# Chunk-selected attention and gated FFN on one core: keys of two heads and rows of a half turned by one DMA each, chunk rows for the last batch only, a new order table

## The chip, the cores and the metric

The kernel runs on one core of a Trainium2 chip. The metric is the device time of one execution in microseconds. Three runs of the kernel before gave 314.94, 315.1 and 316.24 us (median 315.1).

## The reference

Four batches of 8 heads, 768 positions, head dimension 64. The keys of a head are cut into 24 chunks of 32. For each query a bound on its score with each chunk is formed from the chunk's elementwise minimum and maximum; the query keeps the 6 chunks with the largest bounds among those that are causally allowed, and attends to them only. The result of all heads is one row of 512 per position (3,072 rows), which goes through an RMS norm and a gated feed-forward layer with 1,536 hidden units.

```python
k_min = np.min(k_chunks, axis=3)
k_max = np.max(k_chunks, axis=3)
ub = np.sum(np.maximum(q[:, :, :, None, :] * k_min[:, :, None, :, :],
                       q[:, :, :, None, :] * k_max[:, :, None, :, :]), axis=-1)
ub = np.where(causal, ub, -1000000000.0)
top_chunks = np.argsort(ub, axis=-1)[..., -top_k:]
...
scores = np.where(mask, scale * np.matmul(q, k.transpose(0, 1, 3, 2)), -1000000000.0)
attn = softmax(scores)                 # along the keys
x = (attn @ v), heads side by side     # 3072 x 512
xn = x / rms * rms_g
g, val = xn @ w_gate, xn @ w_val
return (g * sigmoid(g) * val) @ w_out
```

(The softmax, the product with `v` and the sigmoid are shortened here.)

## The kernel before

The kernel first makes a list of 1,975 steps (`add`), each with the engines that may run it, the steps it depends on and the buffers that it opens or uses. `order.run` then emits them in the order of the written-out table `ORDER`, whose tokens are step numbers, with a letter where the step runs on another engine than its first choice (`a` ScalarE, `v` VectorE, `g` GpSimd). So every engine's queue, and the sync engine's DMA queue too, is in the order of that table, and nothing passes anything else on its own engine. `SLOTS` says how many buffers of a kind there are.

Heads go in pairs: 16 pairs, four to a batch, pairs 0 to 3 being batch 0. Positions go in tiles of 128, six to a head (`NT`), in two halves of three tiles.

Pairs 0 to 3 are prepared by `early`, the others two at a time by `late`. `late` gets its keys in one of two ways:

- `direct` (batch 1, pairs 4 to 7): the keys come in natural rows (`nat`), TensorE transposes them in fp32 (`turn`, L488, 6 transposes of 128 x 128 a pair), an engine copies the result out of PSUM to `kt`, VectorE reduces it to minimum and maximum of each chunk (`bounds_of`, L675 and L677), `ku` gets their difference, and casts put the transposed keys into the key set `kes` (L269).
- `chunked` (batches 2 and 3, pairs 8 to 15, from `CHUNKED` = 8 on): a second load brings the keys of four heads as one row per chunk (`kc`, L711, 768 KB); VectorE folds the rows down to minimum and maximum (L722, L732); TensorE turns the small result (`kt<-kk`, L749). The keys themselves are laid out as bf16 in `kb` by GpSimd (`kN`, L269) and turned into `kes` by two DMA transposes, one a head (`turned`, L660).

The table of `kb` has one buffer; its gaps hold the rows that add the chunk bias to the score matmul. `qn` is the same for the queries: VectorE writes the chosen chunks into its gaps (`sel`, L540), and two DMA transposes a pair (L660, `qs<-qn`) turn it. The scores `sc` (L859) of a pair wait for its queries and keys; ScalarE takes the exponential (`pt`, L876), GpSimd masks, TensorE multiplies with the values (`av`, L895), VectorE divides (`xb`).

`norm` works on a half of a batch, three tiles of rows. ScalarE or VectorE sums the squares, GpSimd takes the power (`root`). In batches 1 and 2 ScalarE scales a row block into `xf` (L981), which shares two buffers `ob` with the output tiles `osb`, and GpSimd multiplies with the gains (`xs`, L986); in batches 0 and 3 VectorE does both (`xs`, L972). Each `xs` is a bf16 tile of 128 x 512. In batch 0 TensorE transposes it; in the others one DMA transpose for each `xs` (L1000) writes it into `xT`, laid out so that 384 positions stand side by side for each group of 128 features.

`ffn` on a half: 12 gate steps (L1046) and 12 val steps (L1066) of four matmuls 128 x 384 each, which wait for all of the half's `xT`; `tanh` on ScalarE (L1053), two products on VectorE, and 9 output steps `po` (L1086) of four matmuls. `osb` goes out by a DMA on the sync queue (L1101). The weights come by DMAs that GpSimd issues. 48 `busy` matmuls on zeros fill TensorE's waits near the start.

Of the kernel before, what the change touches and what calls it, by code (L numbers as in the profile page):

```python
# [25 lines left out]
    86 134 0 66 54 3 25 12 11 67 50 59 19 58 89 28 55 24 52 38 137 42 133 85 68 69 181 62 63 229 182  # L26
    5 135 7 27 56 64 87 53 2 60 61 230 206 110 207 90a 1 111 99a 98a 18 100a 74 139 136a 51 183 71v
    254 255 73v 76 46 77 70v 138a 88a 26 144g 141 142 148a 145g 94 45 93 231 143g 158 72v 149 147g
    30 184a 189 95g 96g 40 150 190 22 101 13 75a 192a 232a 97a 91 193g 185 102 103 233 104g 241a 6
    208 151 37 237 65 44 146a 186a 234a 112 195a 196a 47 113a 105 240g 9 119a 152g 238 244a 20 210  # L30
    211a 191g 153 106 209a 154 219a 155g 117 197 156 199 114 107g 108 239g 198 120g 157v 115a 245
    109v 629 622 623 619 630 246 620 626 247 615 616 242a 608 609 215a 194g 200g 41 201 140g 159 34
    212 202 627 624 256 257a 612 203g 204 248g 16 605 48 116 606 621 122a 213 258 33 160 205v 631
    161a 249 123g 613 118g 625 124 250 628 243a 251g 92g 187 214g 640 281 252 235 29 260 165 216a
    167g 126 317 125 263a 32 633 617 261 253v 49 15 259a 127g 643 641 267a 644 607 164 657 162 610
    262g 654 311 296 632 168g 658 188g 220 128 614 130g 634 636 650 163v 221 129 655 647 637 651
    266g 642 611 131 121g 289 222 635 645 132v 166g 648 171a 638 639 282 10 283a 618 172-174 409 670
    290a 664 667 671 169g 31 78 674 668 23 345 646 223g 236g 652 360 175g 656 285 659 672 661 649
    665 666 683 677 675 680 176 662 684 36 678 681 264g 318 178g 320 319a 224 669 660 663 177 179
    284 4 321a 653 170g 17 180v 1270a 381 682 1271a 685 268 709 673 679 287 676 218g 226g 710 312  # L40
    1269a 690 21 225 693 227 686 269 270 79 314 694 8 315a 703 304 704 43 696 305a 700 695 706 265g
    691 288 291 228v 687 271g 217g 297 692 313v 729 701 688 697 1272 272 1273 711 689 80 410 735 732
    730 726 14 733 707 727 705 1280 1274 1281 39 698 713 1277 736 1282v 273 274g 708 298a 722 1275
    723 286g 702 719 1278 1276v 737 731 720 338g 716 1279v 728 375 734 275 307 717 712 721 1308 276a
    724 714 1298 310 303 699 752 81 1309 755 738 1293 753 300 756 761 1294 302 295 294 299 754 715
    301g 1310 758 762 1299 292 718 725 82 1300 757 1288 745 763 759 746 742 1303 1295 748 1304 749
    277 83 760 346 306 308g 353 739 764 1305 347a 354a 1289 349 1296 1291 309 743 1301 356 1297 747
    348 1302 750 293g 740 744 741 751 322a 316a 57 1358a 1359a 352 355 1290 1306 1311 1312 1307 1283
    1284 1286 323 351 1292 1360a 1318 1285 1338 1361 1339 1328 1319 1329 325 1323 1324 1287 368 1362
    369a 357g 324 1333 361 1363 1366 1367 1340 326g 1325 1364 1365a 1334 1330 1331 84 1368v 1320  # L50
    1332 1321 1369 1326 1327 1341 1316 1370 373 327 1313 1342 1371a 1336 328 1314 334 329 331g 330g
    332 1315 1322 1317 1335 1395 335 359 333 1372 1392 1373 1375 1397 337g 362a 1337 1393 1417 1374
    1418 1382 1383 1394 1376 1398 1385 384 385a 1396 364 1399 1419 1384 336 382 374 363 358 1377
    1387 1380 1348 1343 1386 1349 1388 1378 1379 411 383a 376 378 278g 370 1381 386a 377a 1389 1350
    365g 350g 379a 380a 395g 340 1344 371 412 372g 773 1351a 413 774 786 769 779 790 770 787 803 776
    425 771 1345 777 279 804 280g 387 805 780 772 791 800 1346a 781 792 801 388 797 778 798 775 431
    794 795 765 766 1412 802 782 788 783 1413 367 389 428 429a 426 434 435a 390v 391 793 427a 767
    799 339 839 784 1414 796 840 417 818 392 832 414g 402g 789 806 398 366 393 768 475 833 394g 834
    819 432 433a 807 808 430a 1400 1401 809 785 459 397 824 396 821 1420 825 836 1415 815 816 399
    1421 1390 1391 810 1407 817 826 837 341 1416 822 838 418g 1408 828 842 811 829 845 401g 846 400  # L60
    1409 820 843 1402 1403 460 812 478 415 830 841 416a 884 436v 1404 1405 823 479a 813 847 1352 476
    477a 403 844 831 342g 835 848 343 849 404 814 874 875 525 827 1406 437 885 876 1347 438 850 439
    860 445g 863 864 405 461 866 1353 861 853 867 851 440g 441 865 878 854 879 862 870 868 1410 886
    871 887 881 888 1422 1411 882 880 480a 462 855 481 929 877 889 852 442 531 930 883 857 858 1427
    1423 1424 912 913 926 856 923 924 344g 419 872 420 859 873 443 444g 447 446 1354 869 902 908 448
    927 914 452g 909 1355 903 920 915 895 1356a 931 1425 890 463 925 896 905 916 921 904 1430 897
    917 891 918 1432 906 1426 1428 899 922 1357 892 928 900 406g 919 1429 893 1433 910 509 898 894
    1431 907 901 1434 1437 954 1435a 1436 449 464g 465 941 958 484 932 965 495g 421 911 1449v 451g
    1448a 482 407 450 1447a 959 1450 485v 1438 944 947 942 966 1451 1452 955 483v 486v 1453 1439 948
    528 454 466v 960 943 945 526 937 1455 1456 962 1440v 956 938 963 487 964 1458 961 1441 1536a 933  # L70
    510 532 455 529v 489 1459 946 488 534 1454 533a 957 934 939 1442 950 968 951 971 1443 511 408g
    512 949 535a 972 940 1444 967 527v 935 936 422g 1457 490g 1460 467 952 953 969 491 1537a 970
    456v 973 1481 424 492 1445a 493 1494 1538a 1539 1540 1516-1518 494g 1491 1492 423 1446 453 468g
    497 470 496 1493 1466 1467 1495 1506 1484 1482 1483 1507 1509 1508 1469 502g 1541 1544 1468 1470
    536a 1010 996 997 1499 1510 1485 1496-1498 1542 471 1000 1461 998 1545 1486 469 1462 1547 1548
    1546 1543 1549 1487 974 1500 1488 1011 1489 457 1519 1490 1001 975 1464 498 1463 517 976 983
    1511 1007 984 1512 1008 989 999 990 1013 499 1476 1012 1002 1477 1465 1501 979 1014 991 500 1009
    501g 504 1017 1513 1520 1015 1478 1502 1503 1004 1504 1005 992 977 993 978 472g 1031 1003 980
# [105 lines left out]
def kernel(  # L184
# [973 lines left out]
```

## Time and profile before

| | |
|---|---|
| median of three runs | 315.1 us |
| the profiled execution's own time | 315.06 us |
| its span | 313.2 us |
| mean granted TensorE clock | 0.987 |

The profile is of one execution. A span is the time from the first to the last instruction; the execution's own time also has what lies around it (1.9 us here). In the slices each digit is the busy share of a fortieth of the span, 7.83 us. A group's row has line, engine, operation, output and inputs, count, then busy us, mean ns of one, and the idle time before it with what ended it. A "SPq" row is an instruction of the sync engine's DMA queue: its duration is the time that issuing took, not the transfer. In the list of DMA issues the last number is the median time from issue to landing.

### The profile page before, as it was taken

To read this page: it belongs to the slowest core of one execution; us is meant where nothing else is said; L and a number is where in the kernel's file an instruction comes from. 1 tells how busy PE (TensorE), PEld (TensorE's weight loads), DVE (VectorE), ACT (ScalarE), POOL (GpSimd) and SP (SyncE) were. 2 spreads that over 40 slices of the span, in tenths; PEclk is the share of its full clock that TensorE was granted. 3 is DMA by queue.
4 is the path that set the end of the run, shared out by engine and by line. 5 is a ranking of instruction groups with operands and counts; after the bars stand their busy time and mean duration, and the time that the engine had idled before them with its cause. 6 is when DMAs were issued, how large, how long until landed. Compare 5 with 4: busy or idle time off the path is not lost.

```text
span 313.2 us, 8148 instructions
## 1 busy us (share of the span) xinstructions
PE 298.2 (95%) x3045; PEld 190.2 (61%) x3070; DVE 230.4 (74%) x678; ACT 197.9 (63%) x438; POOL 126.8 (40%) x225
## 2 busy tenths in 40 slices
PE   6999999999999996999979999999999999999995
PEld 3677777666677654666646656666665555555542
DVE  6799998999879975599757887767556866753650
ACT  4899999635898974778847656675775331322230
POOL 8567795334466634966522546334320200000000
PEclk9999999999999999899989999999999999999999
DMA  8889899993999999977999449395300221200102
GB/s 168 196 190 215 221 217 207 199 209 59 206 204 183 219 177 238 181 179 148 190 178 208 114 101 184 79 196 126 86 36 0 64 89 34 87 11 22 70 33 100
DMA packets 124823, 44.05 MB, mean 141 GB/s; under 512 B 117616, under 2 KB 121200, under 8 KB 124400
## 3 DMA queue, kind: packets, MB, share of 16 engines
q1 hardware_dynamic: 119504, 38.42, 58.9%
q0 software_dynamic: 3680, 4.72, 8.5%
q10 hardware_dynamic: 1600, 0.39, 0.6%
q8 instruction: 24, 0.39, 0.6%
q14 instruction: 15, 0.12, 0.2%
HBM read 31.72 MB, written 6.29 MB: 121 GB/s over the span
## 4 chain that ended last, share of the span: by engine, by line
PE 77%; DMA 12%; SPq 3%; ACT 3%; DVE 2%; POOL 2%; issue 1%; ACTq 0%; POOLq 0%
PE gp L1046 18%; PE po L1086 18%; PE vp L1066 18%; PE sc L859 8%; PE av L895 4%; PE ub L571 4%; DMA wg<-in_moe_w_gate_dram 3%; PE pq L488 3%; DMA kes<-kb 3%; PE busy L316 2%; DMA out_dram<-osb 2%; SPq L660 2%; DMA vnat<-in_v_dram 1%; PE pk L488 1%; DMA nat<-in_k_dram 1%; DMA nat<-in_q_dram 1%
## 5 line engine op out<-in xcount | busy, mean ns | idle before, releaser
L876 ACT ACTIVATE pt<-sc 128x512 bf16<-128x512 f32 (+3 forms) x192 | 94.3, 552 | 19.7 <-PE sc L859 18.7
L1053 ACT ACTIVATE sg<-gp 128x384 bf16<-128x384 f32 x96 | 45.3, 495 | 54.2 <-PE gp L1046 53.9
L1046 PE MATMUL gp<-xT,wg 128*128 128x384 bf16 x384 | 74.6, 328 | 0.2 <-DMA wg<-in_moe_w_gate_dram 0.2
L1066 PE MATMUL vp<-xT,wv 128*128 128x384 bf16 x384 | 73.6, 328 | 0.0
L1086 PE MATMUL po<-wo,hh 128*128 128x512 bf16 x267 | 68.2, 379 | 1.1
L1058 DVE SCALAR_TENSOR_TENSOR sg<-sg,gp 128x384 bf16<-128x384 bf16 x96 | 51.1, 548 | 22.1 <-ACT sg L1053 21.3
L859 PE MATMUL sc<-qs,kes 89*128 89x128 bf16 (+5 forms) x431 | 58.1, 251 | 3.8 <-DMA kes<-kb 2.5
L1074 DVE TENSOR_TENSOR hh<-vp,sg 128x384 bf16<-128x384 f32 x96 | 51.1, 551 | 12.4 <-PE vp L1066 10.1
L1066 PEld LDWEIGHTS <-wv 128*128 128x128 bf16 x384 | 36.4, 98 | 23.9 <-issue 0.3
L1046 PEld LDWEIGHTS <-wg 128*128 128x128 bf16 x384 | 36.1, 98 | 23.3 <-issue 1.0
L1086 PEld LDWEIGHTS <-hh 128*128 128x128 bf16 x288 | 27.0, 98 | 26.2 <-DVE hh L1074 0.3
L859 PEld LDWEIGHTS <-kes 89*128 89x128 bf16 (+1 forms) x432 | 32.1, 98 | 15.8 <-DMA kes<-kb 3.0
L895 PEld LDWEIGHTS <-pt 128*128 128x128 bf16 x672 | 33.3, 98 | 11.8 <-POOL pt L882 0.6
L882 POOL TENSOR_SCALAR_AFFINE_SELECT pt<-pt 128x256 bf16<-128x256 bf16 (+1 forms) x48 | 27.3, 574 | 31.4 <-ACT pt L876 30.6
L895 PE MATMUL av<-vx,pt 128*128 128x65 bf16 x672 | 39.3, 194 | 0.5 <-POOL pt L882 0.5
L986 POOL TENSOR_TENSOR xs<-xf,gains 128x512 bf16<-128x512 f32 x12 | 15.2, 1270 | 12.9 <-ACT xf L981 12.9
L488 PE MATMUL pq<-ident_f,nat 128*128 128x128 f32 x96 | 16.2, 292 | 4.2 <-ACT pt L876 2.9
L916 DVE TENSOR_TENSOR xb<-av,rden 128x384 bf16<-128x384 f32 (+1 forms) x40 | 19.1, 478 | 1.4
L267 ACT ACTIVATE osb<-po 128x512 f32<-128x512 f32 x14 | 8.5, 604 | 16.6 <-PE po L1086 14.4
L316 PE MATMUL busy<-zeros 128*128 128x512 bf16 x45 | 16.3, 431 | 1.5 <-DVE zeros L311 1.3
L527 DVE MAX8 m<-ubm 128x8 f32<-128x8 f32 (+4 forms) x192 | 16.8, 159 | 0.0
L488 PEld LDWEIGHTS pq<-ident_f,nat 128*128 128x128 f32 x96 | 12.0, 150 | 7.4 <-ACT pt L876 3.0
(97 smaller groups left out, 329.5 us busy)
## 6 DMA issues: line engine op xcount, KB each, us to landing
vnat<-in_v_dram SPq DMA_DIRECT2D x16, 384.0 KB, 4.8
out_dram<-osb SPq DMA_DIRECT2D x24, 256.0 KB, 2.2
nat<-in_k_dram SPq DMA_DIRECT2D x24, 192.0 KB, 4.1
nat<-in_q_dram SPq DMA_DIRECT2D x24, 192.0 KB, 5.0
kc<-in_k_dram SPq DMA_DIRECT2D x4, 768.0 KB, 6.4
nat<-in_k_dram SPq DMA_DIRECT2D x16, 96.0 KB, 3.1
wg<-in_moe_w_gate_dram POOLq DMA_DIRECT2D x2, 768.0 KB, 10.4
wv<-in_moe_w_val_dram POOLq DMA_DIRECT2D x2, 768.0 KB, 10.6
```

The lines of the kernel that those rows point to most:

```text
L316: nc.tensor.matmul(t[:, 0:n], zeros[:, 0:P], zeros[:, 0:n], start=True, stop=True)
L488: nc.tensor.transpose(t[:, j * P:(j + 1) * P], nat.tile[:, x * nb + j0 + j].rearrange("p h d -> p (h d)"), ident_f[:])
L859: nc.tensor.matmul(t[:, x:x + m, :].rearrange("p a b -> p (a b)"), ke[kk, kb * P:(kb + 1) * P], qs[kk, q0 * P:(q0 + m) * P], start=not tri ...
L876: nc.scalar.activation(out=t[:, 0:nn, :], in_=sc.tile[:, 0:nn, :], func=ACT.Exp, scale=SCALE)
L882: nc.gpsimd.affine_select(out=pt.tile[:, 0:nd, :], in_=pt.tile[:, 0:nd, :], compare_op=ALU.is_ge, fill=0.0, base=0, pattern=[[0, nd], [1, ...
L895: nc.tensor.matmul(av.tile[:, qi - i0, :], pt.tile[:, x, :], VX[c.v.slot][:, hl * NT + kb, :], start=(begin and m == 0), stop=(left[0] == ...
L1046: nc.tensor.matmul(t[:], wg[:, g, hs], xt.tile[:, g, :], start=(g == 0), stop=(g == NP - 1))
L1053: nc.scalar.activation(out=t[:], in_=gp.tile[:], func=ACT.Tanh, scale=0.5)
L1058: nc.vector.scalar_tensor_tensor(out=sg.tile[:], in0=sg.tile[:], scalar=1.0, in1=gp.tile[:], op0=ALU.add, op1=ALU.mult)
L1066: nc.tensor.matmul(t[:], wv[:, g, hs], xt.tile[:, g, :], start=(g == 0), stop=(g == NP - 1))
L1074: nc.vector.tensor_tensor(out=t[:], in0=vp.tile[:], in1=tg.tile[:], op=ALU.mult)
L1086: nc.tensor.matmul(po.tile[:], hhs[ht].tile[:, th * P:(th + 1) * P], wo[:, ht, :], start=(ht == 0), stop=(ht == NHT - 1))
```

## The change

- Batch 2 is prepared by `direct` like batch 1; only batch 3 (pairs 12 to 15) keeps the chunk rows.
- In batch 3 the keys of both heads of a pair are turned by one DMA transpose of 128 x 1,536. For that `kb` has the two heads side by side with equal strides, which `blocks` describes.
- The three row blocks of a half share one buffer `xs` (3 x 512 a partition), and in batches 1 to 3 one DMA transpose of 128 x 1,536 turns them, once all three are there. `xT` is laid out by row block first, so the gate and val matmuls read three runs of 128 positions.
- The number of `xs` buffers goes from 3 to 1 (each three times as large).
- The `load=` numbers are for the search that writes the table; they change no instruction.
- The order table is new as a whole: the 1,987 steps stand in another order, and some run on another engine. Its text is left out here.

```diff
-                 m8=2, mx=3, small=6, ubm=2, pt=8, xb=2, xt=3, row=2, xs=3, ff=5, hh=22, ob=2)
+                 m8=2, mx=3, small=6, ubm=2, pt=8, xb=2, xt=3, row=2, xs=1, ff=5, hh=22, ob=2)
...
-    SIDE, CHUNKED = 2, 8
+    SIDE, CHUNKED = 2, 12
...
-    KB = [const.tile([P, 2 * HW + P], BF16, name=f"kb{i}") for i in range(SLOTS["kb"])]
+    KB = [const.tile([P, 2 * NT * P], BF16, name=f"kb{i}") for i in range(SLOTS["kb"])]
...
+    def blocks(x, start, step, n):
+        return bass.AP(x.tensor, x[:, start:start + 1].offset, [x.ap[0], (step, 2), (P, NT), (1, n)])
...
-    def lay(e, out, nat):
-        evict(e, out[:, 0:2 * (HW + D)].rearrange("p (h t d) -> p h t d", h=2, d=P)[:, :, 0:NT, 0:D],
-              nat.tile[:].rearrange("p t h d -> p h t d"))
+    def lay(e, out, nat, whole):
+        evict(e, blocks(out[:], 0, (NT * P if whole else HW) + D, D), nat.tile[:].rearrange("p t h d -> p h t d"))
...
-            c.ke = turned(c, KB, kb, KE, c.ks, "kX", [kn])
+
+            def move(e, c=c, kb=kb):
+                nc.sync.dma_start_transpose(
+                    out=KES[:, c.ks.slot].rearrange("d h (t p) -> d (h t) p", p=P), in_=KB[kb.slot][:])
+
+            c.ke = [add("kX", "SP", 1.4, rank(c.at[0], c.b, "kX"), move, [kn], opens=[c.ks], uses=[kb],
+                        load=120000)]
...
+        xs, xss = Buf("xs", own=o), []
         for j, i in enumerate(rows):
-            xs, tp = Buf("xs", own=o), Buf("ps", "norm")
+            tp = Buf("ps", "norm")
...
             if b:
-                def move(e, j=j, xs=xs):
-                    if xt.tile is None:
-                        tile_of(xt, [P, NP, W], BF16, "xT")
-                    nc.sync.dma_start_transpose(
-                        out=xt.tile[:, :, j * P:(j + 1) * P], in_=xs.tile[:])
-
-                x = add("xT", "SP", 1.3, rank(at, b, "xT", j, pace), move, [x], opens=[xt],
-                        uses=[xs], load=60000)
-                xts.append(x)
                 continue
...
+        if b:
+            def move(e):
+                tile_of(xt, [P, 3, NP, P], BF16, "xT")
+                nc.sync.dma_start_transpose(
+                    out=xt.tile[:].rearrange("p j g q -> p (j g) q"),
+                    in_=xs.tile[:].rearrange("p j d -> p (j d)"))
+
+            xts.append(add("xT", "SP", 1.4, rank(at, b, "xT", 0, pace), move, xss, opens=[xt], uses=[xs],
+                           load=120000))
...
-                    nc.tensor.matmul(t[:], wg[:, g, hs], xt.tile[:, g, :],
+                    nc.tensor.matmul(t[:], wg[:, g, hs], xt.tile[:, :, g, :],
...
-                    nc.tensor.matmul(t[:], wv[:, g, hs], xt.tile[:, g, :],
+                    nc.tensor.matmul(t[:], wv[:, g, hs], xt.tile[:, :, g, :],
```

In the new table the sync queue begins batch 1's end with a chunk load (for pairs 12 and 13), two query transposes, a query load and the output store whose buffer the first `xf` of batch 1 takes; in the old one the store followed a chunk load directly, and two key loads, a value load and a query transpose followed it.

More of the change, by code (lines that the diff above doesn't have):

```diff
@@ L121 @@
+    1979 1901a 1902 1980a 1981 1972-1974 1975v 1976 1982 35 1983 1984 1985a 1986
 """
@@ L379, in copy_e @@
             for x in KB:
[L380 to L381 removed]
+                evict(e, blocks(x[:], D, NT * P - D, D), et.tile[:].rearrange("p (o t) d -> p o t d", o=1).to_broadcast(
                           [P, 2, NT, D]))
@@ L713, in load @@
                 in_=k[b, cs[0].h0:cs[0].h0 + 4].rearrange("h (c t) d -> (h c) (t d)", t=CH))
-        ld = add("kcload", "SP", 0.6, rank(cs[0].lr[0], b, "kcload"), load, opens=[kc], load=700000)
+        ld = add("kcload", "SP", 0.6, rank(cs[0].lr[0], b, "kcload"), load, opens=[kc], load=850000)
         reds, half = [], CH * D // 2
```

208 lines of the change are left out of this document (104 added, 104 removed), and 8 rows, old and new, of the table ORDER.

## The prediction

> **What bounds the kernel now.** I read the page first: busy shares, slices and granted clock.
>
> ```profile
> span 313.2 us, 8148 instructions
> PE 298.2 (95%) x3045; PEld 190.2 (61%) x3070; DVE 230.4 (74%) x678; ACT 197.9 (63%) x438; POOL 126.8 (40%) x225
> PE   6999999999999996999979999999999999999995
> PEclk9999999999999999899989999999999999999999
> DMA  8889899993999999977999449395300221200102
> ```
>
> TensorE is busy 95% of the span. Its slices are full except the first, the last and two in the middle: slice 16 ("6", from 117 us) and slice 21 ("7", from 157 us). At or behind both the granted clock drops, and DMA is full. So elsewhere the time is TensorE's own work, and only those two places can be won back. The windows view gives their price: length, then busy us (x count) of PE, PEld, DVE, ACT and POOL, then the granted clock, DMA share and GB/s.
>
> ```profile
> 116.00:125.00 9.00, 5.46 (x41) 3.69 (x41) 5.37 (x12) 4.84 (x12) 2.88 (x4) 0.95 0.98 229
> 125.00:132.00 7.00, 6.95 (x117) 4.65 (x117) 3.37 (x7) 5.47 (x13) 6.28 (x9) 0.82 1.17 196
> 155.00:161.50 6.50, 4.47 (x49) 2.87 (x45) 5.61 (x13) 4.65 (x10) 1.24 (x3) 1.00 1.20 171
> 161.50:166.00 4.50, 4.21 (x22) 2.63 (x24) 0.00 (x0) 1.34 (x3) 2.17 (x4) 0.62 0.91 217
> 166.00:176.00 10.00, 9.21 (x126) 6.12 (x133) 8.07 (x16) 6.25 (x15) 4.17 (x6) 1.00 0.76 155
> ```
>
> Lost at the first place: idle 9.00 - 5.46 = 3.54 and 0.05, clock 5% of 9.00 = 0.45 and 18% of 7.00 = 1.26, together 5.3 us. At the second: idle 2.03, 0.29 and 0.79, clock 38% of 4.50 = 1.71, together 4.8 us. Both: 10.1 us.
>
> What ended those waits stands in the waits (total us, times, longest), the chain of waits and the timelines.
>
> ```profile
> PE pq L488 <- ACT pt L876: 2.9, 1, 2.9
> PE sc L859 <- DMA kes<-kb: 2.5, 2, 2.3
> ...
> 116.85 6.27 DMA out_dram<-osb
> ...
> 116.38 0.38 SPq L711 DMA_DIRECT2D kc<-in_k_dram  x1
> ...
> 119.77 4.99 SPq L660 DMA_TRANSPOSE qs<-qn  x1
> ...
> 156.13 2.65 SPq L660 DMA_TRANSPOSE qs<-qn  x1
> ...
> 123.23 0.72 ACT L981 ACTIVATE xf<-xb,ri 128x512 f32<-128x512 bf16 x1 [3.43 <-DMA out_dram<-osb]
> ...
> 161.73 0.50 PE L859 MATMUL sc<-qs,kes 89*128 89x128 bf16 x3 [2.26 <-DMA kes<-kb]
> ...
> out_dram<-osb SPq DMA_DIRECT2D x24, 256.0 KB, 2.2
> kc<-in_k_dram SPq DMA_DIRECT2D x4, 768.0 KB, 6.4
> qs<-qn SPq DMA_TRANSPOSE x24, 2.8
> xT<-xs SPq DMA_TRANSPOSE x18, 2.5
> kes<-kb SPq DMA_TRANSPOSE x16, 2.8
> ```
>
> First place: the 768 KB chunk load is issued at 116.38, and an output store behind it lands after 6.27 us instead of the median 2.2. ScalarE's `xf` needs the buffer that this store reads and waits 3.43 us; the exponentials queue behind it, and TensorE waits 2.9 us for one. A query transpose held the sync queue for 4.99 us. Second place: another held it 2.65 us, the key transpose behind that was late, and the scores of pair 11 (batch 2) waited 2.26 us. Both are backlog on the one sync queue and the DMA engines.
>
> **The change, part by part.** *Batch 2 without chunk rows* adds fp32 key transposes to TensorE: 4 pairs x 6 = 24.
>
> ```profile
> 51.80 0.69 PE pk L488 x6
> ...
> L749 PE MATMUL kt<-ident_f,kk 96*128 96x96 f32 x8 | 1.4, 251 | 0.0
> L675 DVE TENSOR_REDUCE kmx<-kt 128x12 f32<-128x384 f32 x16 | 8.6, 534 | 1.2 <-ACT kt L265 1.2
> L269 POOL CAST kes<-kt 64x384 bf16<-64x384 f32 x25 | 12.6, 507 | 2.4 <-ACT kt L265 1.5
> L269 POOL CAST kb<-nat 128x768 bf16<-128x768 f32 x8 | 6.7, 842 | 11.4 <-issue 5.6 <-DMA kes<-kb 3.9 <-DMA nat<-in_k_dram 2.0
> L265 ACT ACTIVATE kt<-pk 128x384 f32<-128x384 f32 x16 | 7.6, 491 | 1.3 <-PE pk L488 1.2
> ...
> 0.00:313.20 313.20, 15.51 (x32) 0.99 0.69 141
> ...
> 0.00:313.20 313.20, 10.67 (x8) 0.99 0.69 141
> ```
>
> In the chain six transposes take 0.69 us: 24 x 0.115 = 2.8. Half of the eight `kt` transposes go, 4 of them, between 0 (all overlapped) and 4 x 0.251 = 1.0; I take 0.4. TensorE: +2.4 us, on the bound, since nothing hides work on a full engine. The last two rows are the windows view of the whole span for the cascade L732 and the fold L722: 26.2 us of VectorE, half of which goes (-13.1). Back come 16 reductions, 8 of L675 and 8 of its twin L677, at 0.54 (+8.6) and some evictions; ScalarE gets up to 8 evictions of 0.491 (+3.9); GpSimd 16 half casts of 0.507 less 4 of 0.842 (+4.7). VectorE, ScalarE and GpSimd are 74, 63 and 40% busy, and in the 116 to 176 stretch no fuller than these rows show: cost 0 beside TensorE. Were that cover gone, +4.7 on GpSimd would be the most.
>
> DMA: two loads of 768 KB go, 1.57 MB, or 6.9 us at the 229 GB/s of the stretch at 116. Batch 2's keys no longer pass the sync queue as 8 transposes, so the wait of the second place has no such transfer left to wait for.
>
> *One DMA where two or three stood* (keys of batch 3, rows of a half).
>
> ```profile
> L1000 SPq DMA_TRANSPOSE xT<-xs x18: 1188/1212/2576, 126.0 to 269.2; - x18
> L660 SPq DMA_TRANSPOSE kes<-kb x16: 1209/1283/3319, 109.3 to 217.1; - x16
> ...
> L986 POOL TENSOR_TENSOR xs<-xf,gains 128x512 bf16<-128x512 f32 x12 | 15.2, 1270 | 12.9 <-ACT xf L981 12.9
> L972 DVE SCALAR_TENSOR_TENSOR xs<-xb,ri,gains 128x512 bf16<-128x512 bf16 x12 | 8.8, 752 | 0.9 <-POOL ri L964 0.9
> 173.71 0.65 PE vp L1066 x4
> 300.03 1.73 PE po L1086 x8
> ```
>
> An issue takes 1.21 us at 512 columns and 1.28 at 768 (minimum/median/maximum ns), so nearly the same for either; at 1,536 I take 1.3, at most 2.6. Transposes issued fall from 58 to 34 (24 queries, 4 keys, 6 rows): at least 24 x 1.21 = 29 us of sync-queue time is free. Landing at 1,536 columns was never seen. From below: 2.5 us at 512 and 2.8 at 768 add 0.3 for 256 columns, so 2.8 + 0.9 = 3.7. From above, in proportion: 2 x 2.8 = 5.6. I take 3.7, since the two rows show mostly a fixed time.
>
> But the gate matmuls now wait for a transfer that starts after the third row. Needed from the start of the last `xs`: 1.27 (GpSimd) or 0.75 (VectorE) + 1.2 + 3.7 = 6.2 or 5.65. Against it stands the TensorE work that the changed program puts between that `xs` and the half's first gate, by its order and the rows (gate or val 0.65, po 0.87). The shortest are batch 3's first half, 3 gates, 3 vals and 1 po = 4.8; batch 1's first, 4 po and 1.5 of scores and values = 5.0; batch 2's first, 5 po, 1 val, 1 gate and 0.2 = 5.8. The others have 7.7 or more. Short by 0.85, 1.2 and 0.4: 2.5 us of new waiting. The kernel before had 4.1 us there (batch 3's first half: 3 vals, 2 gates, 1 po) against 0.75 + 1.2 + 2.5 = 4.45 and shows no such wait, so 2.5 is rather high; I let the excess stand for small waits elsewhere. Bounds: 0, and 14 (the slower rival).
>
> *Gates read three runs of 128 columns* instead of 384 in a row, and the `blocks` layouts write the same elements: 0. The masks' matmuls, which repeat one block of 128, and the gates take the same.
>
> ```profile
> L865 PE MATMUL sc<-trimask,ident_b 128*128 128x384 bf16 x16 | 5.2, 327 | 0.0
> L1046 PE MATMUL gp<-xT,wg 128*128 128x384 bf16 x384 | 74.6, 328 | 0.2 <-DMA wg<-in_moe_w_gate_dram 0.2
> ```
>
> *The new order.* The store that frees the buffer for the first `xf` of batch 1 had 2.8 us of TensorE work before that `xf` (2.8 + 3.43 waited is about its 6.27); now it has 5.9. A landing as late as before would leave 0.4. The first gate stands behind the same TensorE work as before (29.4 and 29.7 us without the fillers), so the start is worth 0. One `xs` buffer of three rows instead of three single ones: the next half's rows come over 10 us later, 0.
>
> Sum: 313.2 - 10.1 + 2.4 + 2.5 = 308.0 of span. The profiled execution took 315.06 with 1.9 around its span, and the median is 315.1, so the two agree: **309.9 us**.
>
> The Trainium skill, "TensorE: Matmul & The Clock Gate", section "What's actually happening", halves the clock only after an idle window of about 3.4 us. By that rule waits of 2.9 and 2.26 us would not have cost clock, only 6.7 of the 10.1 would be theirs, and the sum would be 313.3. The rows above disagree (0.82 and 0.62 right behind them), and the measurement decides; it gets no chance.
>
> **The rivals.** *A: no new wait* (the covers suffice, as 4.1 against 4.45 did): 307.4. *B*: the forecast. *C: one of the two stalls comes back.* For it: the changed order still puts a 768 KB chunk load and then transposes ahead of that store, and a queue that backs up can do so elsewhere. Against: 24 fewer transposes and 1.57 MB less. It keeps about 5: 314.9. *D, slower: the merged row transpose.* It lands in proportion to its columns, 5.6 us. Needed 8.1 or 7.55: short by 2.3 to 3.1 at the three halves named and by 0.7 together at the rest, 9 in all, and three waits above 2 us cost clock like the 4.50 us row, 1.7 each: 14 instead of 2.5, 321.4. It makes the kernel slower (316.7) once the new waits reach 9.3. For it: twice the columns in one transfer; against: 2.5 and 2.8. *E: the change doesn't do what it says*: both stalls stay or move, TensorE's 2.4 are added: 317.5.
>
> **How the numbers follow.** A 0.15, B 0.50, C 0.17, D 0.09, E 0.09. The likeliest is B. Its own range is 307.4 (A's value) to 312.4 (twice its new waits). The range for 8 in 10 goes from 306.8, a little below A, to 317.5, E's value, and leaves out D. What a measurement here can tell from no change is about 0.5%, 313.5 to 316.7. Faster: A, B and a quarter of C = 0.70; same: half of C and B's edge = 0.11; slower: D, E and a little of C = 0.19.
>
> **What would show it.** Right: no slice below 9 between the first and the last, PEclk 9 throughout the middle, `out_dram` never 6 us in the chain, `xT` and `kes` landing near 3.7, 24 more fp32 transposes on TensorE. Wrong: a TensorE wait on `xT` above 1 us at several halves (D), a sync-queue issue of several us with a dip of the clock (C, E), or gates above 0.65 us for four.

## The result and the profile after

The changed kernel takes 310.06 us (median of four runs, 309.95 to 310.92) beside 315.02 us of the kernel before on the same chip: 0.9842 of its time, 95% interval 0.981 to 0.9874. The forecast was 309.9. Two executions of one run below, over 1.5% above its fastest, stand in its median and not in its ratio.

The page of the kernel after (span, busy shares, TensorE's slices, its granted clock, DMA):

```profile
span 308.3 us, 8187 instructions
PE 299.6 (97%) x3090; PEld 191.0 (62%) x3090; DVE 234.3 (76%) x688; ACT 197.1 (64%) x434; POOL 134.0 (43%) x233
PE   7999999999999999989999999999999999999995
PEclk9999999999999999999999999999999999999999
DMA  7799999849999999599996445275310210610102
```

Both dips of TensorE are gone, and those of the clock with them. One slice of 8 is left, the 18th. The same five windows as before (length; busy us and count of PE, PEld, DVE, ACT, POOL; clock, DMA share, GB/s):

```profile
116.00:125.00 9.00, 9.00 (x90) 6.55 (x88) 7.99 (x14) 7.57 (x20) 6.26 (x8) 1.00 1.04 194
125.00:132.00 7.00, 5.86 (x49) 2.95 (x47) 6.86 (x12) 6.62 (x15) 6.17 (x8) 1.00 0.60 68
155.00:161.50 6.50, 6.50 (x84) 4.78 (x83) 5.18 (x11) 4.81 (x11) 3.30 (x5) 1.00 1.08 205
161.50:166.00 4.50, 4.50 (x42) 2.64 (x41) 4.26 (x10) 3.18 (x8) 4.50 (x7) 1.00 0.92 148
166.00:176.00 10.00, 10.00 (x143) 6.83 (x142) 9.60 (x31) 7.40 (x20) 5.48 (x8) 1.00 0.48 107
```

TensorE stood idle 6.70 us in them before (3.54 + 0.05 + 2.03 + 0.29 + 0.79) and 1.14 us now, all between 125 and 132.

How did the first stall go? The chunk load ahead of it is still there and is as large as before. It now leaves at 105.66 instead of 116.38. The sync queue, the landing of the store that stands behind it (minimum/median/maximum, one transfer), and ScalarE's first `xf`:

```profile
105.66 0.84 SPq L712 DMA_DIRECT2D kc<-in_k_dram  x1
...
113.92 0.53 SPq L1113 DMA_DIRECT2D out_dram<-osb  x1
...
DMA to landing us min/median/max: 5.1/5.1/5.1
...
119.13 0.72 ACT L990 ACTIVATE xf<-xb,ri 128x512 f32<-128x512 bf16 x1 [0.47 <-POOL kes L269]
```

The store is still late: it lands 5.1 us after its issue (6.27 before), at 119.0. But it was issued 5.2 us ahead of the `xf` that needs its buffer, and no wait on it is left in the profile. Nor are small transfers quicker in general: the query transposes land after 3.3 us in the median, 2.8 before. The second stall went because its transfer went: the keys of pair 11 no longer come by a DMA transpose.

The waits (us in total, times, longest) name the one that the change brought, which ends in the next window:

```profile
PE gp L1058 <- DMA xT<-xs: 0.9, 1, 0.9
```

The chain of waits of the same kernel (start, us, what):

```profile
126.06 1.40 POOL xs L996
...
127.49 4.87 DMA xT<-xs
...
132.41 2.77 PE gp L1058 x16
```

GpSimd ends the third row block of batch 1's first half at 127.46, the one transpose is issued at 127.49 and the gates start 4.87 us later, 0.9 us after TensorE had nothing else to do (from 131.5, so about half of the 1.14 us is this). It is the only half at which a merged transpose is waited for. It lies in the slice of 8 (from 131.0 us). The transpose's own line (minimum/median/maximum of the issue in ns, then of the landing in us):

```profile
L1029 SPq DMA_TRANSPOSE xT<-xs x6: 1286/1444/2891, 127.5 to 262.0; - x6
...
DMA to landing us min/median/max: 3.7/4.3/5.0
```

From the list of DMA issues, the merged transposes of keys, with the median landing last:

```profile
kes<-kb SPq DMA_TRANSPOSE x4, 3.8
```

The sync queue's timeline at the first place, as it is now (start, us spent on issuing, line, what, how many):

```profile
116.90 3.41 SPq L661 DMA_TRANSPOSE qs<-qn  x2
...
127.49 1.44 SPq L1029 DMA_TRANSPOSE xT<-xs  x1
```

Between 121.4, the end of a value load's issue, and 127.49 the queue issues nothing and stands waiting for the rows; in the kernel before it was held from 119.77 to 124.76 by one query transpose. Last, the group of the key transposes on TensorE, 24 more than before:

```profile
L490 PE MATMUL pk<-ident_f,nat 128*128 128x128 f32 x72 | 11.8, 277 | 0.0
```

### The profile page after: what moved, and what is told of

Its sections match the earlier page's. It is cut to its first block, busy times and chain, and to the rows that moved or that the text cites. A ratio compares the mean times of both kernels' runs of the same rounds, so it can differ in the third digit from the quotient of the medians.

```text
span 308.3 us, 8187 instructions
## 1 busy us (share of the span) xinstructions
PE 299.6 (97%) x3090; PEld 191.0 (62%) x3090; DVE 234.3 (76%) x688; ACT 197.1 (64%) x434; POOL 134.0 (43%) x233
## 4 chain that ended last, share of the span: by engine, by line
PE 87%; DVE 5%; POOL 3%; DMA 3%; ACT 1%; issue 0%; ACTq 0%; DVEq 0%; POOLq 0%
PE gp L1058 20%; PE vp L1078 20%; PE po L1098 18%; PE sc L866 10%; PE av L902 5%; PE ub L573 4%; PE pq L490 3%; PE busy L319 3%; PE pk L490 2%; DMA xT<-xs 2%; POOL xs L996 1%; DMA nat<-in_q_dram 1%; DVE xs L981 1%; POOL pt L889 1%; PE sc L872 1%; ACT junk L951 1%
## 5 line engine op out<-in xcount | busy, mean ns | idle before, releaser
L1078 PE MATMUL vp<-xT,wv 128*128 128x384 bf16 x384 | 74.5, 326 | 0.0
L1098 PE MATMUL po<-wo,hh 128*128 128x512 bf16 x288 | 72.1, 379 | 0.0
L866 PE MATMUL sc<-qs,kes 89*128 89x128 bf16 (+5 forms) x432 | 57.3, 249 | 0.9 <-ACT pt L883 0.9
L902 PEld LDWEIGHTS <-pt 128*128 128x128 bf16 x672 | 34.3, 98 | 12.8 <-POOL pt L889 1.3
L889 POOL TENSOR_SCALAR_AFFINE_SELECT pt<-pt 128x512 bf16<-128x512 bf16 (+1 forms) x48 | 28.4, 599 | 29.2 <-ACT pt L883 28.9
L902 PE MATMUL av<-vx,pt 128*128 128x65 bf16 x672 | 40.5, 194 | 0.0
L269 POOL CAST kes<-kt 64x384 bf16<-64x384 f32 x42 | 21.8, 524 | 7.1 <-ACT kt L265 5.7
L971 POOL TENSOR_TENSOR ri<-ms,mhalf 128x3 f32<-128x3 f32 x8 | 7.0, 872 | 39.3 <-DVE ms L964 37.1
```

The costliest lines, as they stand in the source:

```text
L866: nc.tensor.matmul(t[:, x:x + m, :].rearrange("p a b -> p (a b)"), ke[kk, kb * P:(kb + 1) * P], qs[kk, q0 * P:(q0 + m) * P], start=not tri ...
L889: nc.gpsimd.affine_select(out=pt.tile[:, 0:nd, :], in_=pt.tile[:, 0:nd, :], compare_op=ALU.is_ge, fill=0.0, base=0, pattern=[[0, nd], [1, ...
L902: nc.tensor.matmul(av.tile[:, qi - i0, :], pt.tile[:, x, :], VX[c.v.slot][:, hl * NT + kb, :], start=(begin and m == 0), stop=(left[0] == ...
L1078: nc.tensor.matmul(t[:], wv[:, g, hs], xt.tile[:, :, g, :], start=(g == 0), stop=(g == NP - 1))
L1098: nc.tensor.matmul(po.tile[:], hhs[ht].tile[:, th * P:(th + 1) * P], wo[:, ht, :], start=(ht == 0), stop=(ht == NHT - 1))
```

## The experiments

How the two stalls went is clear from these views; which part of the change is worth what is not: it removes bytes (1.57 MB), removes transfers, and puts everything in a new order, all at once. Each batch of runs had its own runs of the kernel before, with medians from 314.4 to 315.7 us, so ratios are compared, not times. A ratio is not the quotient of the two medians and can differ from it by up to 0.3%.

### The order alone

Three tables of the kernel before, each with one or two steps moved. *Store first*: the output store that the first `xf` of batch 1 waits for goes ahead of the chunk load.

```diff
 sync queue at 115 us
-  chunk load, output store, key loads, value load, query transpose
+  output store, chunk load, key loads, value load, query transpose
```

> The kernel before with one step moved: the output store whose buffer the first xf of batch 1 takes is issued ahead of the 768 KB chunk load instead of behind it. Theory (order on the sync queue): the store then lands in about 2.5 us instead of 6.27, the wait of 3.43 us on ScalarE and the 2.9 us of TensorE behind it go, and with them the low clock: 5.3 us less by the windows, at most 1 of it given back elsewhere, so 310 to 311 us. Rival (the DMA engines are full there, whatever the order): the load comes 0.5 us later and the fold of its rows waits instead; 314 us or more.

Measured 314.15 us, 0.9938 (0.9916 to 0.996). Its waits:

```profile
PE gp L1064 <- DMA xT<-xs: 2.8, 1, 2.8
PE sc L877 <- DVE sg L1076: 2.2, 1, 2.2
PE sc L877 <- DMA kes<-kb: 2.2, 1, 2.2
```

Its windows at the first place, and VectorE at the second (in brackets its wait):

```profile
116.00:125.00 9.00, 8.19 (x128) 5.80 (x127) 5.31 (x11) 7.60 (x16) 5.46 (x7) 1.00 1.02 230
125.00:132.00 7.00, 4.51 (x51) 2.77 (x48) 6.83 (x11) 4.73 (x14) 7.00 (x8) 1.00 0.99 185
...
165.68 1.45 DVE L740 TENSOR_TENSOR kd<-kc 96x1024 f32<-96x1024 f32 x1 [5.42 <-DMA kc<-in_k_dram]
```

The wait on the store is gone, and 2.8 us on the row transposes stand in its place: idle in the two windows is 0.81 + 2.49 = 3.30 where it was 3.59, but this wait goes on to 133.09, and with the window from 132 to 140 idle is 4.39 (3.59 before). The query transpose behind the chunk load still took 5.40 us to issue. The stall was handed to the next user of the queue. What gained is not idle time. The clock stayed at 1.00, but that is not all of it: eight runs of the kernel before on the same chip had 1.00 too and took 315.0 us in the mean, and the eight runs of this table with 0.999 or 1.00 took 314.0.

The 2.2 us on VectorE's `sg` show a second way in which the chunk load can stall TensorE. At the second place VectorE comes to the fold of the chunk rows before they have landed and stands 5.42 us, and `sg` is the next step in its queue. In the kernel before VectorE stands 5.34 us there as well, and TensorE waits only 0.25 us for `sg`, since it comes to that step 2.3 us later (167.7 instead of 165.4).

*Query load later* moves a query load of the second place behind the key transposes, and *both* does the two together.

```diff
 sync queue at 153 us
-  query load, key tr., query tr., key tr., chunk load, query load, 2 key tr.
+  key tr., query tr., key tr., query load, chunk load, query load, 2 key tr.
```

> The kernel before with one step moved: the two query loads of a later pair, issued at 153.61 us ahead of pair 11's key and query transposes, are issued behind them. Theory (order on the sync queue): the key transpose at 158.82 us goes out 1.2 to 2.5 us earlier, the scores of pair 11 wait 0 to 1 us instead of 2.26, no low clock follows: 3.5 to 4.8 us less, 310.5 to 312 us. Rival (total load): the transposes are held by the packets ahead of them anyway; less than 1 us, 314 us or more.

> Both moves. Theory: the two gains add, since the stalls are 40 us apart: 8 to 10 us less, 305 to 307 us, which is below the changed kernel (310) because it has no added key transposes. Rival (total load): 313 us or more. If the first move shifts what follows by 4 us against the DMA engines, the second may win less: 308.

Measured 318.24 us, 1.0062 (1.0024 to 1.0099), and 316.53 us, 1.0036 (1.0001 to 1.007). All three theories of the order were missed. The times lie in the ranges of their rivals, which are open upwards, but neither side expected tables slower than the kernel before. The sync queue of the first of these two at the second place:

```profile
160.93 6.87 SPq L678 DMA_TRANSPOSE kes<-kb  x2
```

The two key transposes behind the chunk load (issued at 159.28) took 6.87 us to issue (4.65 before), and the scores waited for keys 4.3 us in all. The transfers that stand behind the bytes wait, whichever they are.

### One part of the change alone, and its opposite

*Rows merged*: the kernel before with one transpose for the three row blocks of a half, at the place of the third; its order is otherwise the old one.

```diff
+        xs, xss = Buf("xs", own=o), []
...
-            xs, tp = Buf("xs", own=o), Buf("ps", "norm")
+            tp = Buf("ps", "norm")
...
+                tile_of(xt, [P, 3, NP, P], BF16, "xT")
+                nc.sync.dma_start_transpose(
+                    out=xt.tile[:].rearrange("p j g q -> p (j g) q"),
+                    in_=xs.tile[:].rearrange("p j d -> p (j d)"))
```

> The kernel before with the row transposes of a half merged into one of 128 x 1,536 (at the place of the last of the three in the queue), one xs buffer and gates that read three runs; all else as before. Forecast's price: the transfer lands in about 3.7 to 4.5 us, new waits 0 to 2.5 us, 12 fewer issues of 1.2 us; 313 to 317 us. Slower rival D: about 5.6 us or more and waits at three halves, 14 us: above 321 us. If strided gate reads cost, four gate matmuls show more than 0.65 us.

Measured 314.45 us, 0.9943 (0.9915 to 0.9972): as expected, and the slower rival D of the prediction falls, since even without a new order only one half waits for its rows:

```profile
PE pq L506 <- ACT pt L894: 2.3, 1, 2.3
PE sc L877 <- DVE sg L1081: 2.2, 1, 2.2
...
PE gp L1069 <- DMA xT<-xs: 1.3, 1, 1.3
```

The first stall (`pq` waits 2.3 us for an exponential) stays, without loss of clock. The wait for `sg` is VectorE's again, which stands 3.29 us for chunk rows just before; the clock is 0.83 over the ten microseconds from 166.

*Rows split*: the kernel after with three transposes of 512 columns for each half, each standing in the table right behind its own row block.

```diff
-            xts.append(add("xT", "SP", 1.4, rank(at, b, "xT", 0, pace), move, xss, opens=[xt], uses=[xs],
-                           load=120000))
+            for j in range(3):
+                xts.append(add("xT", "SP", 1.3, rank(at, b, "xT", j, pace), lambda e, j=j: move(e, j), [xss[j]],
+                               opens=[xt], uses=[xs], load=60000))
```

> The changed kernel with the one row transpose of a half split again into three of 128 x 512, each issued right behind its own rows; all else as changed. Theory (merging is a small part, as the run with only the merge, 0.6% below the kernel before, says): the 0.9 us wait on xT goes, 12 more issues of 1.2 us are paid on a sync queue that is no longer full: 309 to 312 us. Rival (the merge is what freed the queue): the long issues and a TensorE wait above 2 us come back, 313 us or more.

Measured 324.16 us, 1.0278 (1.0227 to 1.0328), far above the theory's range. It lies in the rival's, which is open upwards, and the rival's wait above 2 us is there. Its waits:

```profile
PE sc L886 <- DMA qs<-qn: 5.4, 2, 3.1
PE av L922 <- POOL pt L909: 5.3, 2, 3.4
```

Its sync queue at the first place:

```profile
120.59 1.19 SPq L1050 DMA_TRANSPOSE xT<-xs  x1
121.88 1.23 SPq L681 DMA_TRANSPOSE qs<-qn  x1
...
124.17 5.72 SPq L1050 DMA_TRANSPOSE xT<-xs  x2
129.94 1.34 SPq L476 DMA_DIRECT2D vnat<-in_v_dram  x2
```

The first row transpose stands at the head of the sync queue until its row block is there (120.57), and a query transpose behind it is issued at 121.88; in the kernel after both query transposes were out by 120.31. Its scores waited 3.1 us. The value loads behind the other two rows leave at 129.94, the first of them at 120.98 in the kernel after; GpSimd's masks (`pt`) queue behind its copy of those values, and TensorE waits for them.

That run mixed the number of transfers with their place. *Split in place* keeps the three transposes, but puts all of them where the merged one stands.

> The kernel after with a half's rows turned by three transposes of 512 columns instead of one of 1,536, all three issued at the place of the merged one in the sync queue (18 instead of 6 issues; nothing left out). It separates the number of transfers from the place that the kernel with rows split behind their own row blocks (324.2 us) mixed up. Theory of place (those early issues wait for a row at the head of the queue and hold value and query loads behind them; the number itself costs only queue time, 2 x 1.2 us more a half): the wait of 5.4 us on a query transpose and of 5.3 us on the values goes, rows wait 1 to 3 us once or twice, 310 to 313.5. Rival, the number (twelve more issues fill the queue as before): the stall at 117 to 132 us comes back whole, issues of over 5 us and idle TensorE of 4 us and more, 315 to 324.

Measured 311.3 us, 0.9903 (0.9866 to 0.9939), and no wait above 1.3 us. Its sync queue:

```profile
117.29 3.85 SPq L681 DMA_TRANSPOSE qs<-qn  x2
...
122.33 9.27 SPq L1050 DMA_TRANSPOSE xT<-xs  x3
```

The 9.27 us are three issues, each with its wait for a row; nothing that TensorE needs at once stands behind them, and the query transposes are out before. So the place made nearly all of the loss of the run before: the theory of place held, and the rival above, though its time came, was wrong. The twelve more issues by themselves come to 0.9903 beside 0.9842, a difference (about 1.9 us) that the two intervals only just allow to be chance.

### The bytes

*Chunk loads halved*: the kernel before, old order, all 58 transposes, but each of the four chunk loads brings 384 KB; the minimum and maximum are taken over that half of a chunk.

```diff
-                out=tile_of(kc, [ROWS, CH * D], FP32, "kc")[:],
-                in_=k[b, cs[0].h0:cs[0].h0 + 4].rearrange("h (c t) d -> (h c) (t d)", t=CH))
+                out=tile_of(kc, [ROWS, CH * D], FP32, "kc")[:, half:],
+                in_=k[b, cs[0].h0:cs[0].h0 + 4].rearrange("h (c t) d -> (h c) (t d)", t=CH)[:, half:])
```

> The kernel before with chunk loads of half the size (384 KB instead of 768; minimum and maximum are taken over half of each chunk, so the choice of chunks differs): as many bytes less as the change saves, nothing else changed. Theory (backlog of bytes on the DMA engines): each of the two loads that stand at the stalls lets go 0.39 MB, 1.7 us at 229 GB/s, the long transpose issue at 119.8 us falls from 5.0 to about 3.3, and 2 to 4 us are won: 311 to 313 us. Rival (the number of transfers and their order, not the bytes): less than 1 us, 314 us or more.

Measured 310.92 us, 0.9868 (0.9833 to 0.9902), just below the theory's range. Half the bytes of these loads are worth 1.3%. The chain of waits, the sync queue and the first of the windows at the first place:

```profile
116.75 4.32 DMA out_dram<-osb
...
119.49 3.03 SPq L660 DMA_TRANSPOSE qs<-qn  x1
...
116.00:125.00 9.00, 7.89 (x112) 5.22 (x111) 6.74 (x13) 7.19 (x15) 4.94 (x6) 1.00 1.05 240
```

The store lands after 4.32 us instead of 6.27, the query transpose behind it is issued in 3.03 instead of 4.99, and the first stall shrinks from 3.59 to 1.30 us idle (0.19 of it from 125 to 132) and costs no clock. At the second place idle hardly shrinks, from 3.11 to 2.58 us, with 1.8 us on keys: the key transpose waited for there is issued before that place's chunk load (158.82 and 160.20 in the kernel before). What is gained there is the clock, 1.00 as well. VectorE, too, stands for chunk rows 2.4 us in all where it was 5.9; this run does not separate that from the late small transfers.

It does not show that the bytes which the change saves are its gain. This run saves as many, 1.57 MB, but in other places. The program gives the loads at 31.95 and 86.35 to batch 2 and those at 116.38 and 160.20, at the two stalls, to batch 3. The change drops the first two and keeps the other two whole; this run halves all four. No run dropped the first two alone, or tried the new order alone.

*Rows merged and loads halved* puts that together with the merged rows.

> The kernel before with two of the parts that were tried alone put together: one row transpose a half (alone 314.45, -0.6%) and chunk loads of 384 KB instead of 768 KB (alone 310.92, -1.3%). Left out: half of each chunk's positions in its minimum and maximum, which are taken over the other half alone. Theory A, both feed one backlog, and once it is gone nothing more can be had: 309 to 311, no better than the bytes alone by more than 1.5 us, TensorE's idle time under 9 us, clock 1.00. Rival B, the two are worth their sum (-1.9%): 308 to 309.5. Rival C, the merged transpose brings waits of its own on the rows where no new order was made for it: 311 to 313 with xT waits of 1 us and more.

Measured 309.37 us beside 314.5, 0.9834 (0.9798 to 0.9871), clock 1.00, one wait on `xT` of 1.2 us. It lies within A's and B's ranges both, and its interval holds the product of the two alone (0.9868 x 0.9943 = 0.9812) as well as the bytes alone, so which of the two is right stays open. What it shows is that these two edits, in the old order, take the time down as far as the whole change, by another way: the change does not halve the loads at the stalls.

*After, with halved loads* takes the bytes of batch 3's two chunk loads down as well; its minimum and maximum are over half of each chunk.

> The kernel after with its two remaining chunk loads (batch 3) at 384 KB instead of 768 KB. Left out: half of each chunk's positions in the minimum and maximum of batch 3, taken over the other half alone. Theory: no backlog is left in the kernel after (TensorE idle 8.7 us, most of it at the start and the end), so 0.79 MB less are worth nothing: 309.5 to 310.5, the issues of 3.4 and 5.4 us shorter but no wait of TensorE gone except perhaps the 0.9 us on xT. Rival: the bytes still cost, and half of the remaining chunk loads brings a third of what the change brought, 308 to 309.

Measured 308.65 us, 0.9813 (0.978 to 0.9846). The time lies in the rival's range, but that batch's kernel before was 0.5 us faster too, and the interval overlaps that of the kernel after: whether 0.79 MB less are worth 1 us is open; the 0.9 us on `xT` is still there in its waits, as in those of the kernel after.

*Another queue* asks what is full: the sync queue, or the DMA engines behind every queue. It is the kernel before with its chunk loads issued by GpSimd.

```diff
-            nc.sync.dma_start(
+            nc.gpsimd.dma_start(
                 out=tile_of(kc, [ROWS, CH * D], FP32, "kc")[:],
```

> The kernel before with its four chunk loads of 768 KB issued by GpSimd, on the queue that also brings the weights, instead of by the sync engine, at the same places of the program (nothing left out; same bytes, same order of everything else). It asks whether the backlog is one of the sync queue (a 768 KB load ahead of small transfers in the same queue) or of the DMA engines, which are full whichever queue the bytes stand in. Theory of the queue: the store and the transposes behind the load no longer wait for it, the store that the first row scaling of batch 1 waits for lands near its median of 2.2 us, issues of 5 us go, both stalls go: 308 to 311. Rival, the bytes: the DMA engines are as full as before at 116 us and at 160 us, the wait on the store or on a transpose stays at 2 us or more, 313 to 316; GpSimd's own work behind the issue (masks, value casts) may start later and add 1 to 2 us.

Measured 320.49 us beside 314.43, 1.0209 (1.0172 to 1.0246). Its chain of waits at the two places:

```profile
120.82 5.11 DMA out_dram<-osb
...
161.12 6.19 DMA kes<-kb
```

Its window at the second:

```profile
161.50:166.00 4.50, 0.51 (x3) 0.07 (x1) 1.87 (x4) 1.15 (x3) 0.00 (x0) 1.00 1.10 237
```

The chunk load no longer stands ahead of the store in its queue, and the store still lands after 5.11 us. A key transpose issued at 161.12, three microseconds after a chunk load on the other queue (158.16), lands after 6.19, and TensorE works 0.51 of 4.50 us. While it waits the DMA engines move 237 GB/s. So the theory of the queue falls: bytes in another queue delay these transfers as well, and the backlog is of the DMA engines. The rival held, but came out some us above its range. Part of that was lost elsewhere: from 90 to 110 us TensorE is idle 1.69 us (0.11 before), and the clock is 0.83 from 100 to 110. On the sync queue the load at least keeps what is issued behind it from competing with what is ahead; that reading is argued, not shown.

### TensorE's added work

*Keys twice*: the kernel after with the fp32 key transposes of batch 2 done twice, so that 24 more stand where the change put 24.

```diff
-            for j in range(3):
+            for j in range(6 if w == "k" and c.b == 2 else 3):
+                j = j % 3
```

> The changed kernel with each fp32 key transpose of batch 2 done twice into the same place (24 more on TensorE). Theory (TensorE is the bound there): 24 x 0.115 = 2.8 us more, 312.5 to 313.2 us, so the change paid about the 2.4 us of the forecast. Rival (they lie in waits that are left): less than 1 us more, 310 to 311 us.

Measured 310.12 us, 0.9833 (0.9802 to 0.9865), the time of the kernel after. Its chain of waits at the first and the last of five groups, then the same of the kernel after:

```profile
84.46 0.69 PE pk L491 x6
...
99.75 0.69 PE pk L491 x6
```

```profile
84.91 0.36 PE pk L490 x3
...
98.89 0.36 PE pk L490 x3
```

From the first of these groups to the last the distance is 15.29 us instead of 13.98: 1.31 us for four groups, 0.109 us a transpose. In its place such work costs its full price. But at 132 us the wait of 0.9 us on the row transpose is gone from that kernel's waits, and so is one of 0.6 us for an exponential at 126; the spans end 0.3 us apart (308.6 and 308.3). Work that stands ahead of a wait shortens it. The account closes only in part: 24 transposes are 2.6 us, the two waits 1.5, and 0.45 us is a lead that this execution had already at 78 us, before any of the added work.

### The clock

*Waits made*: the kernel after with four waits of different lengths in the last stage, where no transfer is late: a gate or val step first reads a tile that GpSimd writes 300 to 2,800 columns wide.

```diff
+    STALLS = [(73, 300, ('gate', 82)), (72, 1000, ('val', 75)), (84, 1800, ('val', 87)), (87, 2800, ('val', 93))]
```

> The changed kernel with four waits put into TensorE's last stage, some 8 us apart: a val or gate step first multiplies a copy that GpSimd makes of a just finished tanh tile, of about 1.1, 1.8, 2.7 and 3.8 us. What does a wait cost beside itself? If the clock falls behind every wait above 2 us, as in the kernel before, the two long ones are followed by about 1.7 us of lost clock each: 9.4 + 3.4, 323 us. If it is a matter of where the wait lies against a window of some 3.4 us that runs on its own, only the longest is sure to be followed by it: 319.5 to 321.5 us, with full clock behind the 1.1 and 1.8.

Measured 324.18 us in a single execution, span 322.5; that is above both expectations (323, and 319.5 to 321.5). Its timeline has the waits in brackets; the two shorter ones, 1.26 and 1.96 us, are left out:

```profile
281.47 0.22 PE L958 MATMUL vp<-qn,zeros 128*128 128x128 bf16 x1 [3.08 <-POOL qn L1171]
291.31 0.26 PE L958 MATMUL vp<-qn,zeros 128*128 128x128 bf16 x1 [3.56 <-POOL qn L1171]
```

Waits of 1.26, 1.96 and 3.08 us left the clock at 1.00; only the longest, 3.56 us, was followed by half clock. The four are 9.9 us of the 14.2 us that the span grew (322.5 - 308.3); the half clock takes most of the rest.

What decides is where a wait lies. The windows view, cut in steps of 3.41 us counted from where the clock first rises (at 8.05 us in the kernel before, 6.98 here), shows it; first the kernel before, then *waits made* (clock last but two):

```profile
120.69:124.10 3.41, 0.93 (x10) 0.62 (x7) 2.33 (x3) 0.87 (x2) 0.07 (x1) 1.00 1.11 273
124.10:127.52 3.42, 3.04 (x48) 2.06 (x56) 0.05 (x1) 3.00 (x7) 2.95 (x4) 0.50 1.27 255
...
276.64:280.05 3.41, 1.75 (x10) 0.79 (x9) 1.33 (x3) 1.47 (x3) 1.01 (x2) 1.00 0.20 77
280.05:283.46 3.41, 1.99 (x13) 1.23 (x13) 1.45 (x3) 0.00 (x0) 1.25 (x3) 1.00 0.20 77
...
286.88:290.29 3.41, 0.82 (x4) 0.29 (x3) 0.00 (x0) 0.49 (x1) 2.57 (x5) 1.00 0.00 0
290.29:293.71 3.42, 2.40 (x8) 1.09 (x8) 1.57 (x3) 0.00 (x0) 0.90 (x2) 0.50 0.00 0
```

In the kernel before the first stall left TensorE idle for 2.48 us of one step, 73% of it, and the next step ran at half clock from its first to its last microsecond: 1.7 us lost. Here the wait of 3.08 us fell across the border at 280.05, with 1.66 us idle on one side and 1.42 on the other, and cost nothing; the one of 3.56 us left 2.59 us of one step idle. The second stall of the kernel before (64% of a step) and the other runs fit. Between the first rise of the clock and the last microseconds, the traces of all fourteen kernels have eleven drops, each beginning on such a step. Ten follow a step in which TensorE was idle for 64% or more; no other step was idle for more than 57%. One does not fit: with another queue the step from 99.08 was idle for 49%, and half clock followed. Why that one came, and why the drop here lasted two steps, to 297.12, stays open.

## Why the prediction was right

**What bounds the kernel** held: between the first and the last slice only the two stalls could be won, and both were.

**The cause of the stalls was right; how the change ends them was right only in part.** "Backlog on the one sync queue and the DMA engines" is the DMA engines: with the chunk loads in another queue the store and the key transpose were late as well, and with half the bytes the store landed 2 us sooner. Moving single transfers hands the wait on. But the prediction set the two loads that go against "the stretch at 116", where they do not stand: the loads at both stalls stay. What ended the first stall is what it says under the new order, more TensorE work between the store and the `xf`: a landing as late as before "would leave 0.4", and the store did land late (5.1 us). What ended the second is, as it says, that batch 2's keys no longer pass the sync queue. How much the bytes saved and the transposes saved add to this is not separated by any run.

**The price of the two stalls, 10.1 us**, was idle 6.7 and clock 3.4. Idle of TensorE over the whole span fell from 15.0 to 8.7 us; 1.1 us of the 15.0 are output matmuls whose records are missing (267 of 288), so by 5.2. The forecast had 6.7 - 2.5 = 4.2 for it. Busy time, with those 1.1 us added, went from 299.3 to 299.6, up by 0.3, where +2.4 of work and -3.4 of clock should have brought it down by 1.0. So the idle part came out 1.0 better and the busy part 1.3 worse, and the span, 308.3 beside 308.0, hit because the two nearly cancel: that part is luck. The idle part itself hides new waits that the forecast had at nothing: two on VectorE, 1.0 and 0.5 us, at 46 and 15 us, against 1.0 us saved on a query load at 5 us. The clock part is the weaker number. Each dip takes 1.7 us of clock when it comes (half of 3.41), but it does not come with every stall of this size: the run with the store first waited 2.8, 2.2 and 2.2 us and kept 1.00. Nor does the time follow it in full. Of 31 runs of the kernel before on one chip, 12 had a mean clock of 0.987 to 0.989, as the profiled one with its two dips, and took 315.9 us in the mean; 8 had 1.00 and took 315.0. On another chip it was 315.0 (5 runs) and 313.6 (4). So two dips, 3.4 us of clock, went with 0.9 to 1.4 us of time, and 3.4 was too much for them. Where the rest of the 1.3 us lies stays open.

**The rule of the clock gate** ("TensorE: Matmul & The Clock Gate", "What's actually happening", in the Trainium skill) was given no chance on the strength of two rows. Waits of 3.08 us without and 3.56 us with half clock agree with its idle window of about 3.4 us; the 2.26 us before 161.5 to 166 in the kernel before do not. The same section lets the window run on its own, so that where a wait lies in it could matter. The steps of 3.41 us above agree with that, but a step need not be idle as a whole: 64% was enough. So the prediction was right to let waits of 2.9 and 2.26 us cost clock, and had no ground to expect it each time.

**The key transposes, +2.4, and the new waits, +2.5**, were each worked out soundly and then added. The first have their price in place (0.109 us each, forecast 0.115). Of the second, one wait came, 0.9 us, at batch 1's first half, for which the forecast had 1.2; the other two halves, forecast 0.85 and 0.4, had none. The sum took no account of extra work that lies ahead of a wait and fills it: with 24 transposes more this wait went to nothing and the time stayed (310.12 us).

**The merged transposes**: landing taken as 3.7, measured 4.3 (3.7 to 5.0) for rows and 3.8 (3.8 to 7.2) for keys; issue taken as 1.3, measured 1.44. Both medians are nearer the lower bound (3.7) than the upper (5.6), so the landing grows much less than in proportion, and D (in proportion, 5.6) was wrong. Gates from three runs of 128 columns take 326 ns each beside 328 before: 0 was right.

**C and E** did not happen. C's ground was real: issues of 3.41 us for two query transposes are still there at 116.90, now with nothing behind them that TensorE needs at once.

## What to carry to other kernels

When a small transfer lands late, count the bytes in flight on all DMA engines at that moment before its place in a queue is changed: here half the bytes of the chunk loads were worth 1.3%, a single step moved forward or back at most 0.6%, and another queue cost 2%. Ask, too, whether the transfer has to land sooner: in the changed kernel the store is nearly as late as before, and costs nothing because it is issued 5.2 us ahead of its user. A transfer that needs several producers is better issued after the last of them than in pieces that stand at the head of an in-order queue and hold back what is behind; whether it is one transfer or three mattered little. In a forecast, work that a change adds ahead of a wait, and that wait, are not simply added: the work fills the wait first.

## What the hardware showed that was not expected

- A DMA transpose of three times the columns takes far less than three times as long: 1.44 us to issue and 4.3 to land at 1,536 columns, 1.21 and 2.5 at 512.
- A queue of another engine does not take bytes out of the way: with the chunk load on GpSimd's queue the store landed after 5.11 us (6.27 before) and a key transpose after 6.19.
- The clock fell and rose in steps of 3.41 us whose borders the stalls did not move. A stall of 2.3 us that left 64% of one step idle was followed by half clock; one of 3.08 us that a border cut in two was not.
